# A three-layer kernel on one core: the first phase recorded as steps and emitted by a list scheduler in the kernel

## The chip, the cores and the metric

The kernel runs on one core of a Trainium2 chip. The metric is the device time of one execution in microseconds (us). Engines: TensorE (PE, with PEld for its weight loads), VectorE (DVE), ScalarE (ACT), GpSimd (POOL) and SyncE (SP), which here issues nearly all DMAs. Each engine takes its instructions in the order in which they stand in its program.

## What is computed

```python
s = scale * matmul(p, k.T);  a = exp(s - max);  p_packed = (a / (sum + 1e-9)) @ v
s = scale * matmul(q, p_packed.T);  x = softmax(s) @ p_packed      # 8 batches, 8 heads, 576 x 64
h = max(max(x @ w1, x @ w2), x @ w3);  x2 = h @ w_out              # 4608 x 512 -> 768 -> 512
h = x2 @ w_in;  g = (a0 + a1 h + a2 h^2 + a3 h^3) / (1 + |b0||h| + |b1|h^2 + 1e-6)
out = g @ w_out2                                                   # 4608 x 512 -> 2048 -> 512
```

The weights arrive as 64-bit floats and are turned into pairs (or singles) of 32-bit floats on the chip ("decode"). Each large product is three matmuls: high x high, high x low, low x high (`mm3`, L60).

## The kernel before, in words

Phase one takes the 8 batches in 4 pairs (`bp`). A pair has 4 **units** `u`: two batches `b2`, two groups `g` of four heads. In `place` (L250) the group is the outer index: units 0 to 3 are (g0,b0), (g0,b1), (g1,b0), (g1,b1). A unit goes through these steps, which are named by letters:

- S (`s_stage`, L339): scores of p against k on PE, their maximum on DVE (L350), the exponent on ACT (L359);
- T (`sum_stage`, `a_stage`, L363 and L372): row sums on POOL, reciprocal on DVE (L370), transposes on PE (L377), copy on ACT;
- V, Z (L381 to L400): product with v on PE, scaled on DVE (`zt`, L393), transposed on PE (L399), copied by ACT into `ppk`;
- s (`s2_stage`, L275): scores of q on PE (L283), transposes and sums on DVE, two products with broadcast operands on POOL (L291, L298), exponent on ACT, and the result split into `a2h`, `a2l`.

`m_stage` (L311) multiplies the packed values of one group, both batches, by one decoded weight piece `wt`; its low part `ml` is made on DVE (L326). `y_stage` (L459) does, for one `f` of 6 and one batch, three products `psy` (12 matmuls of 288 columns each, over both groups): the first is copied from PSUM by ACT (L471), the two others are max-ed in by DVE (L473). Two PSUM buffers serve all of them. The result is split into `hh`, `hl`. So a pair has 36 products. `x2_stage` (L480) then does the second layer, 8 times 36 matmuls a pair, from both batches' six `hh`, `hl`.

Decoding a piece (`decode`, L68) is 4 or 5 passes on DVE, 2 or 3 on ACT and one on POOL. In the first pair 12 pieces for the first layer and 4 for the second are decoded; the 12 are kept in DRAM (`w_scr`) and loaded again for later pairs. In pairs 1 to 3 the 32 pieces of phase two are decoded (512 columns each).

What sets the order: the first pair's units and its first decodes follow a hand-written text (`START`, L522) under a manual schedule. From there on, the loops of L533 call steps for the next pair between products (`between`, `PACK`, `SECOND`), and the framework's own scheduler orders all engines.

Phase two (L627 on) is 9 blocks of 512 tokens by 16 chunks: `h_mm`, the rational function on ACT and DVE, `o_mm`. Its first weight tile `wi_0` has a place of its own, so it is loaded before phase one ends.

Of the kernel before, what the change touches and what calls it, by code (L numbers as in the profile page):

```python
# [25 lines left out]
VC = 6  # L26
# [7 lines left out]
def attn_moe_moe2_kernel(  # L34
# [33 lines left out]
    def decode(pl, raw, n, single, pin):  # L68

        hw, lw = raw[:, :, 1], raw[:, :, 0].bitcast(U32)
        t = pl.tile([128, 768], I32, name="dec_t", bufs=2)[:, :n]
        r = pl.tile([128, 768], I32, name="dec_r", bufs=1)[:, :n]
        keep = 0x7FF00000 if single else 0x7FFFFE00
        ins = dve.tensor_scalar(out=t, in0=hw, scalar1=keep, scalar2=None, op0=ALU.bitwise_and)
        if pin:
            tc.keep_in_program_order(ins)
        if single:
            dve.tensor_scalar(out=r, in0=hw, scalar1=0xFFFFF, scalar2=0x100000, op0=ALU.bitwise_and, op1=ALU.bitwise_or)  # L80
        else:
            dve.tensor_scalar(out=r, in0=hw, scalar1=0x1FF, scalar2=None, op0=ALU.bitwise_and)
        act.activation(t, t, AF.Relu, scale=8.0, bias=reb)
        act.activation(r.bitcast(F32), r, AF.Copy, scale=2.0**-20)
        hi, lo = yield
        rf = lo if single else r.bitcast(F32)
        ins = dve.scalar_tensor_tensor(out=rf, in0=lw, scalar=2.0**-52, in1=r.bitcast(F32), op0=ALU.mult, op1=ALU.add)
        if pin:
            tc.keep_in_program_order(ins)
        hib = hi if hi is not None and hi.dtype == I32 else t  # L90
        dve.scalar_tensor_tensor(out=hib, in0=hw, scalar=-0x80000000, in1=t, op0=ALU.bitwise_and, op1=ALU.bitwise_or)  # L91
        if single:
            w = t
        else:
            w = hw
            dve.tensor_scalar(out=w, in0=hib, scalar1=-0x00800000, scalar2=None, op0=ALU.bitwise_and)
            if hib is t:
                act.copy(hi, t.bitcast(F32))
        pool.tensor_tensor(out=lo, in0=rf, in1=w.bitcast(F32), op=ALU.mult)  # L99

    def load_raw(pl, src, bufs):
        n = src.shape[1]
        raw = pl.tile([128, 768, 2] if wide else [128, 768], I32 if wide else F32, name="w_raw", bufs=bufs)[:, :n]
        nc.sync.dma_start(raw.rearrange("p n w -> p (n w)") if wide else raw, src.bitcast(I32) if wide else src)
        return raw

    class Feed:

        def __init__(self, pl, pieces, bufs, first=0, pin=False):
            self.pin = pin
            self.pl, self.pieces, self.bufs, self.raw, self.half = pl, iter(pieces), bufs, [], []
            for _ in range(first):
                self.load()

        def load(self):
            piece = next(self.pieces, None)
            if piece is not None:
                self.raw.append((load_raw(self.pl, piece[1], self.bufs), piece))  # L120

        def start(self):
            if self.raw:
                raw, piece = self.raw.pop(0)
                gen = decode(self.pl, raw, raw.shape[1], piece[3], self.pin) if wide else None
                if gen is not None:
                    next(gen)
                self.half.append((gen, raw, piece))

        def finish(self, load=True):  # L130
            if self.half:
                gen, raw, (tiles, _, then, single) = self.half.pop(0)
                hi, lo = tiles()
                if gen is not None:
                    try:
                        gen.send((hi, lo))
                    except StopIteration:
                        pass
                elif single:
                    act.copy(lo, raw)  # L140
                else:
                    split(hi, lo, raw, lo_eng="pool")
                if load:
                    self.load()
                if then is not None:
                    then()

        def half_step(self, load=True):
            if self.half:
                self.finish(load)  # L150
            else:
                self.start()

        def step(self):
            self.finish()
            self.start()

# [9 lines left out]
    pool.memset(reb, -REBIAS)  # L167

# [13 lines left out]
    rlow = ctx.enter_context(tc.tile_pool(name="rlow", bufs=1, side="right"))  # L182
    wi_0 = rlow.tile([128, 2, 512], F32R, name="wi_0")
    rstack = ExitStack()
    wp = rstack.enter_context(tc.tile_pool(name="wp", bufs=1, side="right"))
    mp = [rstack.enter_context(tc.tile_pool(name=f"mp{x}", bufs=1, side="right")) for x in range(2)]
    hx = bstack.enter_context(tc.tile_pool(name="hx", bufs=2))


    wt_ready, NWT, NW = {}, 4, 12  # L190

    def wt_tile():
        return wp.tile([128, 2, 512], F32, name="wt", bufs=NWT)

    def w_piece(f, g):

        box = []

        def tiles():
            box.append(wt_tile().rearrange("p a b -> p (a b)")[:, :768])  # L200
            wt_ready[2 * f + g] = box[0]
            return None, box[0]

        def keep():
            nc.sync.dma_start(w_scr[f, g], box[0])
# [12 lines left out]

    def again(n):
        if n is not None:  # L220
            wt = wt_tile().rearrange("p a b -> p (a b)")[:, :768]
            nc.sync.dma_start(wt, w_scr[n // 2 % 6, n % 2])
            wt_ready[n] = wt

    def wo_pieces():

        for m in range(4):
            yield (lambda m=m: (wo_h[:, m], wo_l[:, m])), w_out[m], None, False

    def w2_pieces():  # L230

        for i in range(32):
            box = []

            def tiles(box=box):
                box.append(wt_tile())
                hi, lo = (box[0][:, x] for x in range(2))
                return (hi.bitcast(I32) if wide else hi.bitcast(F32R)), lo.bitcast(F32R)

            def keep(box=box, i=i):  # L240
                nc.sync.dma_start(w2_scr[:, :, 512 * i : 512 * i + 512], box[0])

            yield tiles, w_2[i], keep, False
# [6 lines left out]
    def place(u):  # L250

        bp, g, b2 = u // 4, u // 2 % 2, u % 2
        return 2 * bp + b2, g

    last_load = []

    def load_unit(src, u):

        t = kp.tile([128, 4 * 288], F32, name="kt", bufs=NKT)
        last_load[:] = [nc.sync.dma_start(t, src[place(u)])]  # L260
        return t

    a2p = rstack.enter_context(tc.tile_pool(name="a2p", bufs=1, side="right"))
    kp = rstack.enter_context(tc.tile_pool(name="kp", bufs=1, side="right"))

    ppk = a2p.tile([128, 2, 4, 128], F32, name="ppk")
    NKT = 4
# [4 lines left out]
    def soft_tile():  # L272
        return kp.tile([128, S], F32, name="e", bufs=3)

    def s2_stage(u, qt, done):  # L275

        g, b2 = u // 2 % 2, u % 2
        ps = ps_t.tile([128, 2, 512], F32, name="pst")
        for c2 in range(2):
            for h in range(4):  # L280
                x = 32 * (h ^ b2)
                l = slice(64 * c2, 64 * c2 + 64)
                pe.matmul(ps[x : x + 32, c2, :288], lhsT=ppk[l, u // 4 % 2, u % 4, 32 * h : 32 * h + 32],  # L283
                          rhs=qt[l, 288 * h : 288 * h + 288], start=True, stop=True)
# [117 lines left out]
    class Ahead:  # L402
# [8 lines left out]
        def do(self, what):  # L411
# [35 lines left out]
            elif k == "n":  # L447
                self.low()
# [304 lines left out]
```

## Time and profile before

| | us |
|---|---|
| three runs | 1390.1, 1386.04, 1387.13; median 1387.13 |
| profiled execution | 1383.15, its span 1381.4 |
| phase one, first instruction to first matmul of phase two | 584.5 |
| PE busy | 1310.2, 95% of the span |
| DVE busy | 1048.9, 76% |
| ACT, POOL busy | 803.4 and 230.1 |

The page's time by slices shows where PE is not full: the first slices of 34.5 us each, and thin places in phase one; in phase two the slices read 9. Busy times include the pipelined overlap of neighbours, so the sum over a group of instructions can exceed what the engine spent. The profiled execution lies 4 us (0.3%) under the median of the three runs.

### The profile page before, as it was taken

To read this page: it belongs to the slowest core of one execution; us is meant where nothing else is said; L and a number is where in the kernel's file an instruction comes from. 1 tells how busy PE (TensorE), PEld (TensorE's weight loads), DVE (VectorE), ACT (ScalarE), POOL (GpSimd) and SP (SyncE) were. 2 spreads that over 40 slices of the span, in tenths; PEclk is the share of its full clock that TensorE was granted. 3 is DMA by queue.
4 is the path that set the end of the run, shared out by engine and by line. 5 is a ranking of instruction groups with operands and counts; after the bars stand their busy time and mean duration, and the time that the engine had idled before them with its cause. 6 is when DMAs were issued, how large, how long until landed. Compare 5 with 4: busy or idle time off the path is not lost.

```text
span 1381.4 us, 21521 instructions
## 1 busy us (share of the span) xinstructions
PE 1310.2 (95%) x8496; PEld 1088.3 (79%) x8496; DVE 1048.9 (76%) x1634; ACT 803.4 (58%) x1337; POOL 230.1 (17%) x226
## 2 busy tenths in 40 slices
PE   4488999999999989999999999999999999999998
PEld 2277797889778779988888888888888888888886
DVE  4599866665766584188888978889788898888887
ACT  2355534533543253286867767668676686776765
POOL 2332252434433342000100101001010010100000
PEclk9999999999999999999999999999999999999999
DMA  8556545763763272860100101001010010000000
GB/s 279 182 189 226 196 145 183 226 226 134 251 224 119 104 244 102 320 242 1 61 1 9 54 1 61 1 1 61 1 38 24 0 55 0 18 36 0 32 0 31
DMA packets 51556, 140.85 MB, mean 102 GB/s; under 512 B 5632, under 2 KB 5632, under 8 KB 50688
## 3 DMA queue, kind: packets, MB, share of 16 engines
q1 hardware_dynamic: 51168, 138.96, 30.1%
q8 instruction: 66, 1.08, 0.3%
q10 hardware_dynamic: 288, 0.52, 0.1%
q14 instruction: 34, 0.28, 0.1%
HBM read 99.09 MB, written 40.37 MB: 101 GB/s over the span
## 4 chain that ended last, share of the span: by engine, by line
PE 81%; DVE 6%; DMA 4%; issue 1%; POOL 1%; ACT 1%; SPq 0%; POOLq 0%; DVEq 0%; ACTq 0%
PE po L61 10%; PE po L62 10%; PE po L63 10%; PE psh L62 10%; PE psh L61 10%; PE psh L63 9%; PE psy L61 7%; PE psy L63 7%; PE psy L62 7%; DMA w_scr<-wt 3%; PE pst L321 2%; DVE hm L473 1%; DVE wt L91 1%; DVE ml L326 1%; POOL wt L99 1%
## 5 line engine op out<-in xcount | busy, mean ns | idle before, releaser
L61 PE MATMUL po<-wq_b,gh 128*128 128x512 f32 x540 | 212.3, 393 | 0.8 <-ACT gh L54 0.8
L62 PE MATMUL po<-wq_b,gh 128*128 128x512 f32 x540 | 211.3, 391 | 0.0
L62 PE MATMUL psh<-xl,wi_b 128*128 128x512 f32 x540 | 211.0, 391 | 0.0
L63 PE MATMUL psh<-xh,wi_b 128*128 128x512 f32 x540 | 210.6, 390 | 0.0
L61 PE MATMUL psh<-xh,wi_b 128*128 128x512 f32 x540 | 210.6, 390 | 0.0
L652 ACT ACTIVATE hb<-psh,babs 128x512 f32<-128x512 f32 (+1 forms) x145 | 99.5, 686 | 187.3 <-PE psh L63 187.3
L61 PE MATMUL psy<-a2h,mh 128*128 128x288 f32 x576 | 182.8, 317 | 18.4 <-DVE hm L473 10.6
L63 PE MATMUL po<-wq_b,gl 128*128 128x512 f32 x540 | 181.7, 391 | 0.0
L655 DVE SCALAR_TENSOR_TENSOR hb<-h,babs,hb 128x512 f32<-128x512 f32 (+1 forms) x145 | 108.2, 746 | 96.7 <-ACT h L653 96.5
L63 PE MATMUL psy<-a2h,ml 128*128 128x288 f32 x576 | 173.2, 301 | 8.3 <-DVE ml L326 8.3
L62 PE MATMUL psy<-a2l,mh 128*128 128x288 f32 x576 | 172.8, 300 | 0.0
L61 PEld LDWEIGHTS psy<-a2h,mh 128*128 128x128 f32 x576 | 111.0, 193 | 53.1 <-DVE hm L473 22.1
L58 POOL TENSOR_TENSOR xl<-xr,xh 128x512 fp32r<-128x512 f32 x28 | 36.4, 1299 | 632.5 <-ACT xh L54 632.5
L63 PEld LDWEIGHTS po<-wq_b,gl 128*128 128x128 f32 x540 | 101.3, 188 | 24.0
L61 PEld LDWEIGHTS po<-wq_b,gh 128*128 128x128 f32 x540 | 101.4, 188 | 22.9 <-ACT gh L54 1.2
L63 PEld LDWEIGHTS psy<-a2h,ml 128*128 128x128 f32 x576 | 111.0, 193 | 10.5 <-DVE ml L326 9.5
L62 PEld LDWEIGHTS po<-wq_b,gh 128*128 128x128 f32 x540 | 101.4, 188 | 22.4
L61 PEld LDWEIGHTS psh<-xh,wi_b 128*128 128x128 f32 x540 | 101.4, 188 | 22.1
L62 PEld LDWEIGHTS psh<-xl,wi_b 128*128 128x128 f32 x540 | 101.4, 188 | 21.7
L63 PEld LDWEIGHTS psh<-xh,wi_b 128*128 128x128 f32 x540 | 101.4, 188 | 21.7
L61 PE MATMUL psy<-hh,wo_h 128*128 128x288 f32 x384 | 114.5, 298 | 0.0
L654 ACT ACTIVATE u<-psh,av 128x512 f32<-128x512 f32 (+1 forms) x145 | 113.3, 782 | 1.6 <-DVE gl L58 1.6
(105 smaller groups left out, 2754.0 us busy)
## 6 DMA issues: line engine op xcount, KB each, us to landing
w_raw<-in_w_dram SPq DMA_DIRECT2D x32, 512.0 KB, 3.9
w_scr<-wt SPq DMA_DIRECT2D x32, 512.0 KB, 5.0
wt<-w_scr SPq DMA_DIRECT2D x36, 384.0 KB, 4.1
kt<-in_k_dram SPq DMA_DIRECT2D x16, 576.0 KB, 4.6
vraw<-in_v_dram SPq DMA_DIRECT2D x16, 576.0 KB, 5.9
kt<-in_q_dram SPq DMA_DIRECT2D x16, 576.0 KB, 6.2
w_raw<-in_w_dram SPq DMA_DIRECT2D x12, 768.0 KB, 4.6
x_scr<-hm SPq DMA_DIRECT2D x32, 288.0 KB, 2.5
```

The lines of the kernel that those rows point to most:

```text
L58: e.tensor_tensor(out=lo, in0=src, in1=hi.bitcast(F32), op=ALU.subtract)
L61: pe.matmul(out_ap, lhsT=lh, rhs=rh, start=first, stop=False)
L62: pe.matmul(out_ap, lhsT=lh, rhs=rl, start=False, stop=False)
L63: pe.matmul(out_ap, lhsT=ll, rhs=rh, start=False, stop=last)
L91: dve.scalar_tensor_tensor(out=hib, in0=hw, scalar=-0x80000000, in1=t, op0=ALU.bitwise_and, op1=ALU.bitwise_or)
L99: pool.tensor_tensor(out=lo, in0=rf, in1=w.bitcast(F32), op=ALU.mult)
L321: pe.matmul(ps[c : c + 32, b2, :384], lhsT=ppk[l, bp % 2, 2 * g + b2, 32 * h : 32 * h + 32], rhs=wt[l, 384 * i : 384 * i + 384], start=Tru ...
L326: return lambda: dve.tensor_tensor(out=lo, in0=ps[:, :, :384], in1=hi.bitcast(F32), op=ALU.subtract)
L473: dve.tensor_tensor(out=hm, in0=ps[:, :, :288], in1=hm, op=ALU.max)
L652: act.activation(hb, h, AF.Abs, scale=babs[:, 0:1])
L654: act.activation(u, h, AF.Identity, scale=av[:, 3:4], bias=av[:, 2:3])
L655: dve.scalar_tensor_tensor(out=hb, in0=h2, scalar=babs[:, 1:2], in1=hb, op0=ALU.mult, op1=ALU.add)
```

## The change

All of phase one up to the last pair's third-layer input is no longer issued as it is written. Each step is recorded by `add(engine, us, fn, r, w, up, mode, kb)`: an engine, a duration, a function that issues its instructions, what it reads and writes, and a rank. `Plan.run` then picks step after step, under a manual schedule: of all engines the one whose next step can start first by the recorded durations, and on it, among steps within a look-ahead of that start, the lowest rank. Evictions from PSUM have their rank lowered (`up=OUT`, `2 * OUT`), so they go first. Steps marked `two` on DVE and POOL are taken as excluding one another. Tiles come from rings (`Buf`); a step can't be issued before the old tile's users are.

```diff
+        def run(self):
+            free = dict.fromkeys(("PE", "DVE", "ACT", "POOL", "SP"), 0.0)
...
+                            t = max(free[e], op.ready)
+                            for b in op.bufs:
+                                s = b.since()
...
+                    near = [(op.rank, t, op) for t, op in found if t <= first + LOOK[e]]
+                    best = (first, *min(near, key=lambda x: x[:2])[1:])
...
+                elif e == "SP":
+                    dma = max(dma, t + 2.0) + op.kb / 406.0
+                    end, free[e] = dma, t + 0.45
+                else:
+                    if op.mode == "two":
+                        t = max(t, held["POOL" if e == "DVE" else "DVE"])
+                        held[e] = t + op.us
+                    end = t + op.us
+                    free[e] = end - 0.08
+                op.fn()
...
+    LOOK = {"PE": 0.1, "DVE": 0.3, "ACT": 0.2, "POOL": 0.1, "SP": 0.1}
...
+            add("DVE", 0.2 + 0.75 * k, low, r=[raw, rb], w=[rb], mode="two")
+            add("DVE", 0.2 + 0.75 * k, sign, r=[raw, tb], w=[tb, key], mode="two")
...
-        bp, g, b2 = u // 4, u // 2 % 2, u % 2
+        bp, b2, g = u // 4, u // 2 % 2, u % 2
...
+        add("PE", 1.6, mm, r=[mh, ml, *a2[0], *a2[1]], w=[ps])
+        if w == 0:
+            add("ACT", 0.65, lambda: act.copy(hm(), ps()[:, :, :288]), r=[ps], w=[hm], up=2 * OUT)
+        else:
+            add("DVE", 0.76, lambda: dve.tensor_tensor(out=hm(), in0=ps()[:, :, :288], in1=hm(), op=ALU.max),
+                r=[ps, hm], w=[hm], up=2 * OUT)
...
+    YS = [[(f, b2) for f in range(6) for b2 in range(2)] for bp in range(NBP)]
+    YS[0] = [(0, 0), (1, 0), (0, 1), (1, 1)] + YS[0][4:]
...
+    START = "P L0 L1 W0 l0 R R W1 l1 S0 S1 T0 T1 V0 V1 s0 s1 L2 L3 W2 W3 l2 l3 R d m S2 S3 T2 T3 V2 V3 s2 s3 R R R d m m"
...
+    with tc.manual_schedule():
+        plan.run()
+    for t, src in ((av, a_in), (bv, b_in)):
+        nc.sync.dma_start(t, src.partition_broadcast(128))
+    dve.tensor_scalar(out=babs, in0=bv, scalar1=-1.0, scalar2=None, op0=ALU.mult)
+    dve.tensor_tensor(out=babs, in0=babs, in1=bv, op=ALU.max)
```

Beside it: a pair's units are ordered by batch, and `m_stage` takes one batch, both groups and both weight pieces of `f`; in the first pair the products of batch 0 for f 0 and 1 stand ahead of batch 1's. The pass that sets a bit of the mantissa with a second operation (L80) loses it; ACT's conversion (L84) adds 1.0 instead. `hm` has 3 buffers instead of 2. `wi_0` loses its own place: all 16 first weights of phase two are loaded into the room that phase one frees. The last pair's second layer and phase two are still ordered by the framework, as is the preparation of `babs` after the plan.

On PE at the start, before: the first product (rows `psy`) stands behind units 0 to 2 in part (`kt,pt` is S; `ident,e` T; `vraw,at` V; `ident,zt` Z; `kt,ppk` s; `wt,ppk` m).

```order
L377 MATMUL pst<-ident,e 96x128 x6
L347 MATMUL pst<-kt,pt 32x288 x8
L388 MATMUL pst<-vraw,at 32x64 x24
L399 MATMUL pst<-ident,zt_111 128x128
L283 MATMUL pst<-kt,ppk 32x288 x8
L321 MATMUL pst<-wt,ppk 32x384 x8
L377 MATMUL pst<-ident,e 96x128 x6
L61 MATMUL psy<-a2h_315,mh 128x288
L62 MATMUL psy<-a2l_316,mh 128x288
```

The same place now:

```order
L475 MATMUL pst<-kt,ppk 32x288 x16
L526 MATMUL pst<-wt,ppk 32x384 x8
L393 MATMUL pst<-kt,pt 32x288 x16
L434 MATMUL pst<-ident,e 96x128 x12
L452 MATMUL pst<-vraw,at 32x64 x24
L460 MATMUL pst<-ident,zt_108 128x128
L452 MATMUL pst<-vraw,at 32x64 x24
L60 MATMUL psy<-a2h_412,mh 128x288
L61 MATMUL psy<-a2l_456,mh 128x288
L62 MATMUL psy<-a2h_412,ml 128x288
```

Units go in twos (x16, x12), batch 0 is whole before the first product, and the product has its low weight part `ml` from the start.

On DVE at the start, now (L266 to L285 are decode; L457 is `zt`; L483, L495 belong to s):

```order
L266 TENSOR_SCALAR dec_t<-w_raw 128x768
L269 TENSOR_SCALAR dec_r<-w_raw 128x768
L457 TENSOR_SCALAR zt_109<-pst,sm 128x128
L723 TENSOR_SCALAR babs<-bv 128x2
L724 TENSOR_TENSOR babs<-babs,bv 128x2
L285 SCALAR_TENSOR_TENSOR dec_t<-w_raw,dec_t 128x768
L278 SCALAR_TENSOR_TENSOR wt<-w_raw,dec_r 128x768
L483 STREAM_TRANSPOSE e<-pst 128x288 x4
```

The two `babs` rows have come here from the third pair (L541 before); their load now stands tenth in SP's queue, behind 6016 KB of p, k, v, q and weight loads.

A little later on DVE, before and then now, where the first two PSUM evictions of products stand (L473, now L551):

```order
L301 STREAM_TRANSPOSE hm<-e 128x576
L473 TENSOR_TENSOR hm<-psy,hm 128x576
L87 SCALAR_TENSOR_TENSOR wt<-w_raw,dec_r 128x768
L58 TENSOR_TENSOR a2l_587<-hm,a2h_586 128x576
L76 TENSOR_SCALAR dec_t<-w_raw 128x768
L80 TENSOR_SCALAR dec_r<-w_raw 128x768
L473 TENSOR_TENSOR hm<-psy,hm 128x576
```

```order
L285 SCALAR_TENSOR_TENSOR dec_t<-w_raw,dec_t 128x768
L507 TENSOR_TENSOR a2l_589<-hm,a2h_587 128x576
L504 STREAM_TRANSPOSE hm<-e 128x576
L551 TENSOR_TENSOR hm<-psy,hm 128x576 x2
L507 TENSOR_TENSOR a2l_625<-hm,a2h_612 128x576
L559 TENSOR_TENSOR hl_638<-hm,hh_627 128x576
L531 TENSOR_TENSOR ml<-pst,mh 128x768 x2
```

In both, nearly all of the four units' DVE work stands ahead of these rows; now the next two `ml` follow at once.

## Rows read from the trace of the kernel before

**Rows 1.** Stretches by stage: start, first products, pairs' products and second layers.

```profile
core 0: us, PE busy (x) PEld busy (x) DVE busy (x) ACT busy (x) POOL busy (x), PEclk, DMA share, GB/s
0.00:34.80 34.80, 14.84 (x211) 7.85 (x212) 14.45 (x31) 10.23 (x22) 7.49 (x21) 1.00 0.87 279
34.80:68.60 33.80, 13.39 (x181) 7.65 (x178) 19.18 (x36) 10.45 (x18) 9.93 (x15) 0.94 0.53 183
68.60:163.50 94.90, 84.72 (x904) 69.33 (x910) 86.91 (x121) 50.93 (x84) 27.86 (x29) 0.97 0.64 211
163.50:205.50 42.00, 42.00 (x359) 39.13 (x341) 28.29 (x45) 16.49 (x24) 20.93 (x14) 1.00 0.42 145
205.50:290.50 85.00, 81.79 (x910) 67.68 (x916) 53.76 (x94) 38.63 (x72) 28.61 (x34) 1.00 0.59 190
...
332.10:422.50 90.40, 85.97 (x910) 69.69 (x916) 64.82 (x114) 44.50 (x80) 34.21 (x38) 0.96 0.62 203
...
464.10:545.20 81.10, 73.83 (x594) 62.02 (x593) 58.37 (x87) 33.80 (x52) 30.74 (x22) 0.98 0.48 157
545.20:584.50 39.30, 38.36 (x290) 38.15 (x289) 7.19 (x10) 8.44 (x14) 0.00 (x0) 1.00 0.88 314
```

**Rows 2.** The same view for tile psy alone, products of pair 1, then of pair 3.

```profile
205.50:290.50 85.00, 63.33 (x434) 58.06 (x432) 18.23 (x25) 7.64 (x12) 1.00 0.59 190
...
464.10:545.20 81.10, 63.60 (x434) 59.47 (x433) 18.04 (x24) 7.65 (x12) 0.98 0.48 157
```

**Rows 3.** PE's timeline: start us, us, instruction, [idle before it <- who ended that].

```profile
6.34 1.22 PE L347 MATMUL pst<-kt,pt 64*32 64x288 f32 x16 [6.34 <-DMA kt<-in_k_dram]
...
34.88 0.59 PE L61 MATMUL psy<-a2h,mh 128*128 128x288 f32 x1
...
68.63 0.61 PE L63 MATMUL psy<-a2h,ml 128*128 128x288 f32 x1 [6.47 <-DVE ml L326]
...
70.96 0.44 PE L62 MATMUL psy<-a2l,mh 128*128 128x288 f32 x1
...
77.30 0.30 PE L62 MATMUL psy<-a2l,mh 128*128 128x288 f32 x1
...
584.51 0.47 PE L61 MATMUL psh<-xh,wi 128*128 128x512 f32 x1 [0.94 <-DVE hm L489]
```

**Rows 4.** DVE's groups of instructions from 0 to 165.6 us, shapes apart.

```profile
L473 DVE TENSOR_TENSOR hm<-psy,hm 128x576 f32<-128x576 f32 x24 | 18.0, 748 | 2.0 <-ACT dec_t L83 1.0 <-PE psy L63 0.9
L58 DVE TENSOR_TENSOR hl<-hm,hh 128x576 fp32r<-128x576 f32 x12 | 16.0, 1337 | 3.2 <-ACT hh L54 3.1
L80 DVE TENSOR_SCALAR dec_r<-w_raw 128x768 int32<-128x768 int32 x12 | 12.2, 1014 | 0.0
```

**Rows 5.** Timeline around 143 us: DVE and POOL.

```profile
143.15 1.83 POOL L99 TENSOR_TENSOR wt<-wt,dec_t 128x768 f32<-128x768 f32 x1
...
143.28 2.32 DVE L58 TENSOR_TENSOR hl<-hm,hh 128x576 fp32r<-128x576 f32 x1
```

**Rows 6.** DVE's timeline: the same operations when they ran alone.

```profile
70.67 0.55 DVE L80 TENSOR_SCALAR dec_r<-w_raw 128x768 int32<-128x768 int32 x1
...
152.63 0.76 DVE L58 TENSOR_TENSOR hl<-hm,hh 128x576 fp32r<-128x576 f32 x1 [0.27 <-ACT hh L54]
```

**Rows 7.** DMA of the first 60 us: GB/s in 40 slices of 1.5 us.

```profile
GB/s 0 109 293 350 249 339 424 397 348 242 350 424 277 258 182 6 265 304 356 397 243 225 364 410 413 390 70 228 349 240 127 200 196 3 11 225 168 123 391 268
```

**Rows 8.** Waits of PE and PEld (engine, line, waited for: us, times, longest), 205.5 to 584.5 us.

```profile
PEld psy L61 <- DVE hm L473: 18.1, 21, 2.5
...
PE psy L61 <- DVE hm L473: 8.9, 9, 2.3
```

**Rows 9.** ACT's timeline: last of the four casts that phase two's first block needs.

```profile
576.84 0.62 ACT L54 CAST xh<-xr 128x512 fp32r<-128x512 f32 x1
```

**Rows 10.** Groups of instructions whose recorded duration in the plan is shorter.

```profile
L87 DVE SCALAR_TENSOR_TENSOR dec_r<-w_raw,dec_r 128x512 f32<-128x512 uint32 x32 | 27.8, 869 | 9.1 <-ACT dec_r L84 8.8
L58 POOL TENSOR_TENSOR hl<-hm,hh 128x576 fp32r<-128x576 f32 x33 | 47.9, 1451 | 72.7 <-ACT hh L54 68.9 <-DMA w_raw<-in_w_dram 3.5
```

More of the change, by code (lines that the diff above doesn't have):

```diff
@@ L101, in load_raw @@
[L101 to L156, printed above, removed]
@@ L219, in again @@
[L219 to L243, printed above, removed]
+    mp = rstack.enter_context(tc.tile_pool(name="mp", bufs=4, side="right"))
@@ new lines, in s_stage @@
+        add("PE", 0.58, mm, r=[kt, ("pt", 0), ("pt", 1)], w=[ps], mode="t")
+        add("DVE", 0.75, lambda: dve.tensor_reduce(out=mx()[:, 0:2], in_=ps()[:, :, :288], axis=AX.X, op=ALU.max),
+            r=[ps], w=[mx], up=OUT)
+        add("DVE", 0.6, small, r=[mx], w=[mx], up=OUT)
+        add("ACT", 1.38, exps, r=[ps, mx], w=[e, sm], up=OUT)
+        add("POOL", 0.9, sums, r=[sm], w=[sm])
+        add("DVE", 0.2, lambda: dve.reciprocal(out=sm()[:, 4:5], in_=sm()[:, 3:4]), r=[sm], w=[sm])
+        return e, sm
@@ new lines, in x2_out, with x2_store, x2_stage @@
+    def x2_out(b, m, ps, xs):
+        (act.copy if m < 3 else dve.tensor_copy)(xs, ps[:, :, :288])
+    def x2_store(b, m, xs):
+        nc.sync.dma_start(x2_scr[:, m, S * b : S * b + S], xs.rearrange("p a b -> p (a b)"))
+    def x2_stage(b, m, hs):
+        ps, xs = ps_buf("psy"), hm_buf()
+        for half in range(2):
+            add("PE", 2.38, lambda half=half: x2_mm(ps(), m, half, hs),
+                r=[("wo", m), *(x for h in hs for x in h), *([ps] if half else [])], w=[ps])
+        add("ACT" if m < 3 else "DVE", 0.7, lambda: x2_out(b, m, ps(), xs()), r=[ps], w=[xs], up=2 * OUT)
+        add("SP", 0, lambda: x2_store(b, m, xs()), r=[xs], kb=288)
@@ new lines, in attn_moe_moe2_kernel, with m_next, wo_next @@
+    YS = [[(f, b2) for f in range(6) for b2 in range(2)] for bp in range(NBP)]
+    YS[0] = [(0, 0), (1, 0), (0, 1), (1, 1)] + YS[0][4:]
+    m_made = []
+    m_seq = iter([(bp, f, b2) for bp in range(NBP) for f, b2 in YS[bp]])
+    def m_next():
+        got = next(m_seq, None)
+        if got is not None:
+            bp, f, b2 = got
+            m_made.append(got)
+            ms[got] = m_stage(bp, b2, wts[bp, f])
+    wo_seq, w2_seq = iter(range(4)), iter(range(32))
+    def wo_next():
+        m = next(wo_seq, None)
+        if m is not None:
+            decode(raw_ready.pop(("o", m)), False, lambda: (wo_h[:, m], wo_l[:, m]), ("wo", m))
@@ new lines, in attn_moe_moe2_kernel @@
+    loads = [(wi_at(f), f) for f in range(16)] + [(wq_at(f), 16 + f) for f in range(NQA)]
+    per = -(-len(loads) // 8)
+    for b2 in range(2):
+        for m in range(4):
+            for _ in range(min(per, len(loads))):
+                tiles, o = loads.pop(0)
+                load_w2(tiles, o, 1)
+            if (b2, m) == (0, 2):
+                xc = load_x(0, xpa)
+            ps = ps_y.tile([128, 2, 512], F32, name="psy")
+            for half in range(2):
+                x2_mm(ps, m, half, hs[b2])
+            xs = hx.tile([128, 2, 288], F32, name="hm", bufs=3)
+            x2_out(2 * bp + b2, m, ps, xs)
+            x2_store(2 * bp + b2, m, xs)
```

751 lines of the change are left out of this document (417 added, 334 removed), and 3 rows, old and new, of the table SECOND.

## The prediction

> **What bounds the kernel now.** I read the stretches by stage first, since phase two is left alone and only phase one's 584.5 us can move. In [rows 1] the reader takes, for each stretch, its length less PE's and DVE's busy time. In the first two stretches (68.6 us) PE is idle for 40.4 us. In the third, the first pair's products, PE is idle for 10.2 of 94.9 us and DVE works 86.91: here DVE is the bound. In the products of pairs 1, 2 and 3 DVE is idle for 31, 26 and 23 us and PE for 3.2, 4.4 and 7.3: PE is the bound, with holes. In the second layer of a pair (42.0 us) PE has no idle time.
>
> PE's timeline comes next [rows 3]. The first product starts at 34.88 us, stops after a few matmuls, and goes on at 68.63, when the low weight part is there. So 68.6 us pass with less than one of 36 products done. The DVE groups and two pieces of the timeline tell what DVE's time is made of [rows 4 to 6]: a subtraction `hl` takes 0.76 us alone, but 1.337 on average, and 2.32 when it starts 0.13 us after a POOL product of 1.83 us.
>
> **The first pair.** The sum is made on DVE, because it decides when the last product can be finished. Up to 163.5 us it was busy for 14.45 + 19.18 + 86.91 = 120.5 us and idle for 20.4 + 14.6 + 8.0 = 43 us [rows 1]. What does the change do to each?
>
> Work. The order is new, the instructions nearly the same. The pass that loses its second operation gains nothing: it took 0.55 us with two operations when it ran alone [rows 6]; its mean of 1014 ns [rows 4] is waiting for POOL, 12 x 0.46 = 5.6 us in all, and so is 12 x 0.58 = 6.9 us of `hl`. I leave both in. One more piece of the second layer's weight is decoded before the last product (four passes of 0.55 to 0.9 us, [rows 6, 10]: 3 us), and the `babs` rows move here (two small passes, 1 us). Work: 124.5 us.
>
> Idle time. It is bounded below by the first load: PE's first matmul waits until 6.34 us [rows 3], so DVE starts near 8, and above by today's 43 us. I go through the new order. DVE's first 15 rows are some 6.5 us of work. Then stands `babs`, whose load is behind 6016 KB. By the rates of [rows 7], whose slices I add up, that much has landed at 21 us. So DVE is idle for about 15 us by then; without `babs` the row behind it would wait for the second v tile, which lands after some 4.9 MB, near 17 us, and the s step of it, so the wait for `babs` itself costs 2 to 4 us. Next the two units of batch 0 go through s together, and each pass over POOL and ACT leaves DVE with decodes and with batch 1's scores to do; I allow 6 us for the two round trips. For the products proper I take 4 us (8.0 before in 94.9 us). Together 25 us, much nearer to 43 than to 8, because half of the four units' chain cannot be hidden.
>
> So the last product of the first pair ends near 124.5 + 25 = 149.5 us instead of 163.5: **14 us gained**. On the way, the first product should start near 44 us (all of batch 0 stands ahead of it), three are done by 54, and the next waits for `ml`, which on DVE stands behind nearly all four units' work: near 67 us. PE is then idle again and has fallen to the lower level of its clock; the same matmul took 0.44 us at 70.96, after such a wait, and 0.30 at 77.30 [rows 3]. From 67 on, PE needs less than DVE: about 33 products of 63.33 / 36 = 1.76 us [rows 2] and what stood between them, against 78 us of DVE work. Bounds: no gain at all (idle time as before) and 32 us (idle 8 us and some waiting for loads).
>
> **Pairs 1 to 3.** Here PE counts. Pairs 1 and 2 issue the same matmuls; pair 1 took 81.79 us of PE, pair 2 85.97, part of it at the lower clock (0.96 granted over the stretch) [rows 1]. I take pair 1's busy time for both and 2.5 us of holes, since evictions now go first: 84.3 instead of 85.0 and 90.4, so 0.7 and 6.1 gained. Pair 3 has no units to prepare. Its products took 63.60 us of `psy` [rows 2], though they are interrupted half as often as pair 1's 63.33; I take 60, plus 8 for the weight products instead of 73.83 - 63.60 = 10.2, plus 2.5 of holes: 70.5 instead of 81.1, 10.6 gained. At the seams the next products may fill in between second-layer halves; about 1 us a seam, 3 in all. Sum: **20 us**. Bounds: 0, if the holes come back elsewhere, and 28, with no holes and no waits in the weight products.
>
> **Edits at nothing.** `wi_0` is no longer loaded ahead. That puts 512 KB more into the last stretch, which has the DMA engines at 0.88 and moves 314 GB/s [rows 1]: 1.7 us. The fourth input cast of phase two was done at 577.5 and phase two began at 584.5 [rows 3, 9], so 7 us cover it; if that cover is gone, phase two starts up to 2 us late. The third `hm` buffer takes away a wait on stores and adds no instruction. Other pieces of the order on SP only move loads that are issued several us before use.
>
> **The sum** against the profiled execution: 1383.15 - 14 - 20 = 1349. That execution lies 4 us under the median of the three runs, against which I forecast: 1387.1 - 34 = **1353 us**.
>
> **The rivals.** First, no waiting on POOL: if the plan's `two` rule really keeps DVE and POOL apart, the 5.6 + 6.9 us of [rows 4, 6] go as well: 1353 - 12.5 = 1340. For it: the plan knows of the exclusion. Against it: it delays the later step in its own account, and doesn't choose another in its place. The Trainium skill (SBUF — State Buffer, "Who interferes with whom") says that a VectorE instruction with two inputs in SBUF and a GpSimd instruction that reads it hold the shared port in turn, and that the one issued first keeps it for its whole length; the 2.32 us of [rows 5] agree (1.83 less 0.13 waiting, then the own pass). By that rule an order alone saves only what it keeps from meeting.
>
> Second, the first pair doesn't move: DVE is 92% busy in the third stretch, and what is won at the start may be lost to evictions behind decodes. Then only the 20 us are left: 1367. Third, the later pairs don't move, because PE there is nearly full: 1373.
>
> Fourth, on the other side, **evictions come late**. The order is fixed by durations that are too short in places: a decode pass is entered at 0.70 us and took 0.869, a POOL subtraction at 1.25 and took 1.451 [rows 10]. An eviction that stands behind two such passes is late, and with two PSUM buffers a product of 1.76 us leaves only about 1 us over the eviction's 0.748 [rows 2, 4]. Before, PE and its weight loads waited 27 us for these evictions in the last three pairs [rows 8]. The 144 products lose the whole gain when each waits 34 / 144 = 0.24 us longer; at 0.35 us it is 50 us, and 1387 + 16 = 1403. Against it: on the order, evictions stand soon behind their products, and DVE has 23 to 31 us free in each of these pairs.
>
> **Chances.** The forecast's own case 0.50 (1340 to 1364), less waiting on POOL 0.15, only the later pairs 0.15, only the first pair 0.09, late evictions 0.07, no change at all 0.04. Differences within 0.3%, 4 us, are what a measurement of this kernel cannot tell from none. So faster 0.89, same 0.04, slower 0.07. The range from 1331 to 1375 takes in the first three rivals and the bounds of the larger terms; it leaves out the last two cases and the tail of a gain over 56 us.
>
> **What would show it.** First product near 44 us, a gap to about 67, last product of the first pair near 150, with DVE idle for about 25 us until then; pairs 1 and 2 at 84 us of products each and pair 3 near 70; second layers still 41 to 42 us; phase two 797 us long. I am wrong in the first step if DVE's busy time until the first pair's end grows, in the second if PE's holes in the later pairs stay above 4 us each, and wholly if waits of `psy` for `hm` exceed today's 27 us.

## The result and the profile after

| | before | after |
|---|---|---|
| runs, median us | 1386.59 (1385.61 to 1390.1, 4 runs) | 1333.1 (1332.61 to 1333.96, 4 runs) |
| profiled execution, its span | 1383.15, 1381.4 | 1332.61, 1330.4 |
| phase one | 584.5 | 533.4 |
| phase two | 796.9 | 797.0 |
| PE, DVE busy | 1310.2, 1048.9 | 1290.6, 1068.5 |

The ratio after to before is 0.9611 (95% interval 0.9593 to 0.9628): 53.5 us faster, where 34 were forecast. The profiled execution of before lay under its median, so between the two traces there are 51.0 us of span, and all of it lies in phase one. The stretches of the changed kernel, with the columns of [rows 1]:

```profile
core 0: us, PE busy (x) PEld busy (x) DVE busy (x) ACT busy (x) POOL busy (x), PEclk, DMA share, GB/s
0.00:41.20 41.20, 22.31 (x331) 12.25 (x331) 26.36 (x54) 17.47 (x35) 13.73 (x32) 1.00 0.96 316
41.20:65.00 23.80, 16.27 (x158) 11.52 (x151) 19.55 (x32) 9.16 (x14) 9.37 (x6) 0.78 0.75 223
65.00:140.90 75.90, 69.48 (x793) 59.16 (x791) 70.40 (x104) 43.87 (x74) 23.76 (x25) 1.00 0.69 230
140.90:184.80 43.90, 43.33 (x386) 39.58 (x386) 37.83 (x56) 20.73 (x31) 25.60 (x17) 1.00 0.45 146
184.80:263.30 78.50, 78.34 (x878) 66.27 (x876) 61.88 (x96) 39.21 (x72) 31.75 (x35) 1.00 0.73 231
...
303.50:383.80 80.30, 80.30 (x912) 68.99 (x910) 64.09 (x100) 41.14 (x74) 33.36 (x36) 1.00 0.64 204
...
424.10:494.10 70.00, 70.00 (x612) 62.08 (x611) 42.27 (x64) 29.50 (x44) 26.07 (x18) 1.00 0.42 134
494.10:533.40 39.30, 38.39 (x290) 38.16 (x288) 6.45 (x9) 7.63 (x12) 0.00 (x0) 1.00 0.90 320
533.40:1330.40 797.00, 791.63 (x3456) 648.54 (x3456) 673.13 (x1020) 562.34 (x935) 36.91 (x28) 1.00 0.10 33
```

Three things are to be seen. The first pair's products end at 140.9 instead of 162.6 (the stage of [rows 1] is cut a little later, at 163.5), and with its second layer 20.7 us are won by 184.8. From there to 533.4 PE has no idle time worth naming, where before 14.6 us of waits stood in pairs 1 to 3: beside the 8.9 us of [rows 8] mainly these:

```profile
PE psy L61 <- ACT hm L471: 1.7, 2, 1.3
PE pst L321 <- issue: 1.6, 1, 1.6
PE pst L321 <- ACT e L359: 1.1, 1, 1.1
```

And the products of pair 1 take 78.5 us, less than the 81.79 that PE was *busy* with them before [rows 1]. Some of that is only moved: 878 matmuls stand in the stretch instead of 910, because two steps of weight products now come before it (about 1.6 us). Pair 2's products have 912, and take 80.3 us. Pair by pair, with the seam behind it, the time from first product to first product fell from 126.6 to 118.7, from 132.0 to 120.6 and from 120.4 to 109.3 us: 7.9, 11.3 and 11.1.

The first products on PE's timeline (columns as in [rows 3]):

```profile
41.26 0.61 PE L60 MATMUL psy<-a2h,mh 128*128 128x288 f32 x1
...
54.78 0.61 PE L60 MATMUL psy<-a2h,mh 128*128 128x288 f32 x1 [7.44 <-ACT hm L549]
...
60.71 0.53 PE L60 MATMUL psy<-a2h,mh 128*128 128x288 f32 x1
```

The first product starts later than before (41.26 against 34.88), but goes through; one long wait is left, for ACT's copy out of PSUM, and from 60.7 on products follow regularly, where before they resumed at 68.63. On ACT that copy (54.10 us) stands behind the cast of batch 1's `a2h` (L505, 53.52 us), which had waited 2.69 us for DVE's transposition: in this place the plan put an eviction behind another step's chain.

What ended PE's waits from 184 to 534 us (columns as in [rows 8]) is a single row, the first matmul of phase two:

```profile
PE psh L60 <- issue: 1.0, 1, 1.0
```

DVE's groups in the first pair, 0 to 141 us (columns as in [rows 4]):

```profile
L551 DVE TENSOR_TENSOR hm<-psy,hm 128x576 f32<-128x576 f32 x23 | 17.2, 750 | 3.7 <-PE psy L62 3.4
L285 DVE SCALAR_TENSOR_TENSOR dec_t<-w_raw,dec_t 128x768 int32<-128x768 int32 x15 | 14.7, 987 | 0.8 <-ACT dec_t L272 0.8
L266 DVE TENSOR_SCALAR dec_t<-w_raw 128x768 int32<-128x768 int32 x15 | 13.6, 904 | 0.0
L269 DVE TENSOR_SCALAR dec_r<-w_raw 128x768 int32<-128x768 int32 x14 | 12.7, 906 | 0.0
...
L559 DVE TENSOR_TENSOR hl<-hm,hh 128x576 fp32r<-128x576 f32 x11 | 9.9, 903 | 1.3 <-ACT hh L557 1.2
```

Two rows of before, for 0 to 163 us, go with them:

```profile
L58 DVE TENSOR_TENSOR hl<-hm,hh 128x576 fp32r<-128x576 f32 x11 | 15.3, 1390 | 3.2 <-ACT hh L54 3.1
L76 DVE TENSOR_SCALAR dec_t<-w_raw 128x768 int32<-128x768 int32 x14 | 8.8, 630 | 0.6 <-DMA w_raw<-in_w_dram 0.6
```

Eleven subtractions `hl` went from 15.3 us to 9.9, and the first pass of a decode (L76, now L266) from 630 ns to 904. All decode passes together are 59 up to the last product in both kernels, and took 53.0 us before and 54.8 now.

Last, PE's small groups in pairs 1 to 3, first before (205.5 to 584.5 us), then after (184.8 to 533.4); m is the product with a weight piece, the other rows V and S:

```profile
L321 PE MATMUL pst<-wt,ppk 64*32 64x384 f32 x544 | 36.5, 497 | 3.5 <-issue 1.6 <-ACT e L359 1.1 <-PE pst L321 0.9
L388 PE MATMUL pst<-vraw,at 96*32 96x64 f32 x384 | 9.3, 228 | 0.0
L347 PE MATMUL pst<-kt,pt 64*32 64x288 f32 x128 | 7.6, 413 | 0.0
```

```profile
L526 PE MATMUL pst<-wt,ppk 64*32 64x384 f32 x528 | 29.0, 493 | 0.0
L452 PE MATMUL pst<-vraw,at 96*32 96x64 f32 x384 | 7.0, 221 | 0.0
L393 PE MATMUL pst<-kt,pt 64*32 64x288 f32 x128 | 5.7, 413 | 0.0
```

One matmul of m lasts as long as before (497 and 493 ns), the group is a fifth cheaper, though it has 16 matmuls fewer, one step, which now stands ahead of the stretch (0.8 us). So what changed is how many of them run beside each other. This the prediction had not seen. Groups that stand wound into each other are counted twice in these busy times. Counted from each matmul's start to the next instruction's, without idle time, m fell by some 7 us, V by 2.0 and S by 0.9.

### The profile page after: what moved, and what is told of

It is laid out like the page before. It is cut to its first block, busy times and chain, and to the rows that moved or that the text cites. A ratio compares the mean times of both kernels' runs of the same rounds, so it can differ in the third digit from the quotient of the medians.

```text
span 1330.4 us, 21496 instructions
## 1 busy us (share of the span) xinstructions
PE 1290.6 (97%) x8496; PEld 1080.3 (81%) x8496; DVE 1068.5 (80%) x1634; ACT 801.7 (60%) x1337; POOL 243.1 (18%) x226
## 4 chain that ended last, share of the span: by engine, by line
PE 93%; DVE 3%; DMA 2%; ACT 2%; issue 0%; SPq 0%; POOL 0%; ACTq 0%; DVEq 0%; POOLq 0%
PE psy L60 10%; PE po L60 10%; PE po L61 10%; PE po L62 10%; PE psh L60 10%; PE psh L61 10%; PE psh L62 10%; PE psy L62 9%; PE psy L61 9%; PE pst L526 3%; DMA bv<-in_moe_b_dram 1%; PE pst L452 1%; PE pst L393 1%; PE pst L475 1%; DMA vraw<-in_v_dram 1%; PE pst L434 1%
## 5 line engine op out<-in xcount | busy, mean ns | idle before, releaser
L60 PE MATMUL psh<-xh,wi_b 128*128 128x512 f32 x576 | 224.4, 390 | 1.0 <-issue 1.0
L61 PE MATMUL psh<-xl,wi_b 128*128 128x512 f32 x576 | 224.9, 390 | 0.0
L62 PE MATMUL psh<-xh,wi_b 128*128 128x512 f32 x576 | 224.6, 390 | 0.0
L60 PE MATMUL psy<-a2h,mh 128*128 128x288 f32 x576 | 178.8, 310 | 7.5 <-ACT hm L549 7.4
L60 PEld LDWEIGHTS psy<-a2h,mh 128*128 128x128 f32 x576 | 109.3, 190 | 35.7 <-issue 17.8
L60 PEld LDWEIGHTS psh<-xh,wi_b 128*128 128x128 f32 x576 | 108.1, 188 | 24.5 <-issue 1.2
L62 PEld LDWEIGHTS psh<-xh,wi_b 128*128 128x128 f32 x576 | 108.1, 188 | 23.0
L61 PEld LDWEIGHTS psh<-xl,wi_b 128*128 128x128 f32 x576 | 108.1, 188 | 23.0
L53 ACT CAST gh<-u 128x512 fp32r<-128x512 f32 (+1 forms) x145 | 90.7, 626 | 41.6 <-DVE u L801 40.4
L799 DVE SCALAR_TENSOR_TENSOR u<-u,av,h 128x512 f32<-128x512 f32 (+1 forms) x145 | 109.0, 751 | 7.6 <-ACT h L796 7.6
```

What stands on the lines that cost most here:

```text
L53: act.copy(hi, src)
L60: pe.matmul(out_ap, lhsT=lh, rhs=rh, start=first, stop=False)
L61: pe.matmul(out_ap, lhsT=lh, rhs=rl, start=False, stop=False)
L62: pe.matmul(out_ap, lhsT=ll, rhs=rh, start=False, stop=last)
L799: dve.scalar_tensor_tensor(out=u, in0=u, scalar=av[:, 0:1], in1=h2, op0=ALU.add, op1=ALU.mult)
```

## The experiments

My theory after the result: the list order does it, and three of its rules carry it (recorded durations, evictions first, DVE and POOL kept apart). The rivals: the new arrangement of the units, or the early products of the first batch, do it; or DVE's work alone sets the first pair. All edits are made to the changed kernel.

**The same steps, the framework's order.** The steps are issued as they were recorded, and the framework orders the engines.

```diff
-    with tc.manual_schedule():
-        plan.run()
+    for o in plan.ops:
+        o.fn()
...
```

> The same steps in the order in which they are recorded, without a manual schedule: the framework's scheduler orders them, as it ordered nearly all of the kernel before. Batch order, products, buffers and passes are those of the change. Theory, by which the list order makes most of the gain: 25 us or more of the 53 are lost, 1358 to 1387. Rival, by which the new arrangement of the work makes it: within 8 us of 1333.

1380.98 us, ratio 0.9959 (0.9942 to 0.9976). Windows by pair: the first pair's products, its second layer, then pairs 1, 2 and 3.

```profile
0.00:162.30 162.30, 109.31 (x1296) 81.82 (x1297) 130.71 (x208) 78.17 (x132) 54.87 (x66) 0.97 0.71 232
162.30:204.70 42.40, 42.40 (x361) 39.23 (x360) 20.45 (x37) 13.75 (x21) 16.85 (x13) 1.00 0.44 153
204.70:340.60 135.90, 127.17 (x1259) 107.27 (x1258) 88.25 (x150) 55.31 (x97) 51.86 (x51) 1.00 0.62 200
340.60:473.10 132.50, 124.94 (x1256) 106.63 (x1255) 91.31 (x151) 56.47 (x98) 52.45 (x51) 1.00 0.54 176
473.10:581.90 108.80, 107.89 (x876) 98.22 (x874) 48.98 (x69) 36.17 (x55) 24.46 (x17) 1.00 0.54 186
```

Its waits of PE in phase one begin with evictions:

```profile
PE psy L60 <- DVE hm L551: 13.8, 17, 1.8
```

The first pair ends at 162.3, as before the change, pair 1 is longer than before and pair 2 as long; only pair 3 keeps the gain. The new arrangement alone is worth 6 of the 53 us; with the list order come the other 48. In this run the framework also orders the start, which before stood in a hand-written order; how much of the 48 that is in the first pair wasn't tried apart.

**Flat durations.** The list scheduler stays, but each engine has one duration for all its steps.

```diff
+            us = {"PE": 1.2, "DVE": 0.7, "ACT": 0.7, "POOL": 1.3, "SP": 0}[eng]
```

> The plan with one duration for every step of an engine: PE 1.2, DVE 0.7, ACT 0.7, POOL 1.3 us. Ranks, rings, look-ahead and loads stay. Theory, by which the order is good because its times are near the chip's: the holes come back, 10 to 25 us, 1343 to 1358. Rival, by which any order that fills an engine with ready steps and puts evictions first does it: within 5 us, up to 1338.

1363.41 us, 0.9829 (0.9811 to 0.9846): 30 us slower than the change, more than the theory's 25. The loss is spread: the first pair's products end at 149.3 (8.4 later), its second layer takes 47.0, and each later pair 5 to 6 us more. Pairs 2 and 3:

```profile
320.80:447.30 126.50, 120.42 (x1176) 106.30 (x1175) 91.40 (x148) 52.39 (x93) 52.59 (x48) 0.97 0.57 185
447.30:561.70 114.40, 107.70 (x884) 100.14 (x883) 58.85 (x82) 39.25 (x61) 28.82 (x19) 1.00 0.59 207
```

PE is idle for 6 us in each again. So without durations by kind more than half of what the scheduler brings is lost.

**More exact durations.** The POOL steps that were entered too short get their measured times.

```diff
-            add("POOL", 0.1 + 1.7 * k, mul, r=[tb, key], w=[key], mode="two")
+            add("POOL", 0.1 + 1.9 * k, mul, r=[tb, key], w=[key], mode="two")
...
-        e, us = (dve, 0.78) if lo_eng == "dve" else (pool, 1.25)
+        e, us = (dve, 0.78) if lo_eng == "dve" else (pool, 1.45)
...
```

> The plan with POOL's durations as the changed kernel's trace has them: decode products 0.1 + 1.9 k instead of 1.7 k, low parts 1.45 instead of 1.25 and 1.3, the subtraction 1.35 instead of 1.2 us. Theory, by which evictions hardly came late: within 3 us of 1333. Rival, by which too short prices still cost the later pairs something: 4 us or more gained, 1329 or less.

1336.38 us, 0.9634 (0.962 to 0.9649): no gain, 3 us the other way, all of it behind the first pair, whose products end at the same 140.9. Errors of 11 to 16% in POOL's durations cost nothing here; with all kinds alike it cost 30 us.

**Evictions not ahead.** They keep the rank of their place.

```diff
-    OUT = 100000
+    OUT = 0
```

> The plan without priority for evictions: OUT is 0, so each step's rank is its place in the record. Theory, by which evictions that go first close PE's holes: the holes and slow weight products of pairs 1 to 3 come back, and the first pair waits too: 10 to 25 us more, 1343 to 1358. Rival, by which the look-ahead and the times do it and ranks hardly matter: within 4 us of 1333.

1342.32 us, 0.9666 (0.9636 to 0.9696): 9 us lost, just under what the theory said, and in another place. (The four executions lie between 1336.7 and 1343.7, and the profiled one is the longest of them.) The first pair's products end 13 us later, at 154.0, with DVE at 119.9 us of work and idle for 34.1 us instead of 24.6; PE waits there for evictions by DVE, as it did not in the change (last row, columns as in [rows 8]):

```profile
0.00:41.20 41.20, 18.80 (x231) 9.82 (x232) 23.07 (x50) 13.88 (x29) 12.15 (x28) 0.93 0.96 307
41.20:154.00 112.80, 96.54 (x1057) 77.92 (x1057) 96.83 (x145) 60.14 (x98) 34.46 (x37) 0.85 0.66 217
...
PE psy L60 <- DVE hm L551: 7.7, 3, 5.3
```

The first pair's second layer gives some 3 us of it back, and the later pairs run as in the change (119.5, 121.0 and 109.3 us with their seams). There DVE has over 20 us free in each pair, and it seems that an eviction finds it free without a rank.

**DVE and POOL not kept apart in the plan.**

```diff
-                    if op.mode == "two":
-                        t = max(t, held["POOL" if e == "DVE" else "DVE"])
-                        held[e] = t + op.us
```

> The plan no longer takes DVE's and POOL's two-input steps as excluding each other; it computes with times that are too early where they meet. Theory: the account only corrects times, the order hardly moves, and the chip's own waiting is the same: within 5 us of 1333. Rival: knowing of the exclusion is what lowered DVE's busy time in the first pair (116 against 120 us), so DVE's busy time there rises by 5 us or more, and the time to 1340 or more.

1345.96 us, 0.9706 (0.9675 to 0.9737): 13 us lost (four executions from 1342.0 to 1350.3, the profiled one 1343.5), but not where the rule was thought to work: the time is the rival's, its reason is not. The first pair ends at 140.1, as early as with it; DVE works 3.2 us more there (119.5 against 116.3) and is idle for less. Pairs 1 and 2 lose, 7.1 and 5.2 us:

```profile
182.80:308.60 125.80, 121.66 (x1262) 105.98 (x1262) 93.42 (x151) 56.84 (x98) 54.03 (x52) 1.00 0.67 218
308.60:434.40 125.80, 121.66 (x1262) 105.99 (x1261) 93.07 (x151) 56.83 (x98) 53.71 (x51) 1.00 0.56 186
...
PE psy L60 <- ACT hm L568: 4.7, 2, 2.3
PE psy L60 <- DVE hm L548: 4.5, 8, 1.1
```

DVE is no busier than in the change (95.4 and 97.1 us), but PE waits 4.1 us in each for evictions; the last two rows are its waits in all three later pairs. The other 3 us of pair 1 are matmuls that stood ahead of it in the change (1262 against 1228). That the plan then places the evictions of DVE and ACT by times that DVE can't keep is my reading; it wasn't tried apart.

**The first pair's `hl` on POOL.** If DVE's work alone sets the first pair, its end must move with it.

```diff
-            hs[b2][f] = y_end(b2, f, hm, "dve" if bp == 0 or (b2, f) == (1, 5) else "pool")
+            hs[b2][f] = y_end(b2, f, hm, "dve" if (b2, f) == (1, 5) else "pool")
```

> In the first pair the low parts hl are made on POOL instead of DVE, as in the later pairs. DVE was busy for 70.4 of 75.9 us from 65 to 141 us, POOL for 23.8. Theory, by which DVE bounds the first pair: 10 passes of 0.76 to 0.9 us leave DVE, of which 4 to 7 us come through: 1326 to 1329. Rival, by which the two engines' excluding each other eats it (POOL's pass takes 1.45 us): within 2 us of 1333.

1335.55 us, 0.9624 (0.9608 to 0.964): no gain, and not to be told from the change. (The profiled execution, 1339.17, is the longest of the four.)

```profile
0.00:41.20 41.20, 21.38 (x323) 11.92 (x327) 26.17 (x54) 17.39 (x35) 13.57 (x31) 0.90 0.96 314
41.20:145.50 104.30, 88.90 (x944) 72.45 (x937) 87.02 (x124) 54.04 (x88) 49.97 (x43) 0.91 0.67 213
...
L285 DVE SCALAR_TENSOR_TENSOR dec_t<-w_raw,dec_t 128x768 int32<-128x768 int32 x14 | 17.5, 1250 | 0.8 <-ACT dec_t L272 0.8
```

DVE's work to the end of the first pair falls from 116.3 to 113.2 us, POOL's rises from 46.9 to 63.5, and the end comes 4.6 us later, at 145.5. Eleven subtractions left DVE, but only 3 us of work: a decode pass there (L285) went from 987 ns to 1250. The theory of DVE alone falls, by which 1326 to 1329 should have come. That DVE and POOL together set the pair's end is a reading of these rows; no run shows it apart.

**Units in the old order.** Batches alternate again; the plan stays.

```diff
+            i = (0, 2, 1, 3)[i] if k in "LWlSTVs" else i
...
```

> The plan stays, but a pair's units alternate between the batches again (b0, b1, b0, b1), as before the change; at the start the first weight product moves behind all four units' s steps in the record. If the batch order is what shortens the start (rival), the first product comes near 58 us instead of 41, DVE's idle time in the first pair goes back to some 43 us, and the 20 us of the first pair are lost: 1353 us. If the list order makes the gain and the batch order only helps (theory), DVE has other work to take and the loss is 5 to 10 us: 1338 to 1343.

1335.91 us, 0.9636 (0.9617 to 0.9655): less lost than either expectation said. The first product starts at 49.0 instead of 41.3, the first pair's products end at 144.8 instead of 140.9: of nearly 8 us at the start 4 are left at the end. The order by batch is worth some 3 us at most; the two intervals overlap.

**The first batch's products not ahead.**

```diff
-    YS[0] = [(0, 0), (1, 0), (0, 1), (1, 1)] + YS[0][4:]
```

> In the first pair the products alternate between the batches from the start; batch 0's product of f 1 no longer stands ahead of batch 1's first. Theory, by which DVE's work sets the first pair's end: under 3 us, 1333 to 1336. Rival, by which the early products of batch 0 shorten the start: the second product waits for batch 1's whole chain, 5 us or more, 1338 to 1345.

1334.57 us, 0.9631 (0.9611 to 0.965): the first pair ends at 143.4, and the time is not to be told from the change. The losses of this run and of the one before add up to under 5 us; the two edits weren't tried together.

**Other loads at the start.** The second v tile is loaded ahead of a weight piece, and `babs` is made in the last pair, so that DVE doesn't wait for it.

```diff
-    START = "P L0 L1 W0 l0 R R W1 l1 S0 ...
+    START = "P L0 L1 W0 W1 R l0 l1 R S0 ...
...
```

> The load of the second v tile stands ahead of the first q and the second weight piece, and the two small loads with the babs passes are recorded in the last pair. In the changed kernel PE waited 2.5 us for that v tile, and DVE 0.6 us for bv. Theory: the start is a chain of loads and of the first two units, so the first product comes 2 to 3 us earlier than 41.3 us; DVE's work decides the pair's end, so 0 to 3 us come through: 1330 to 1333. Rival, by which each us at the start counts in full or more: 1329 or less.

1338.3 us, 0.9644 (0.9623 to 0.9666): slower by 5 us; both expectations missed.

```profile
0.00:41.20 41.20, 15.24 (x206) 7.09 (x206) 23.22 (x41) 14.07 (x24) 11.70 (x23) 1.00 0.91 293
41.20:146.70 105.50, 93.37 (x1065) 75.87 (x1066) 94.70 (x148) 56.51 (x98) 33.66 (x39) 0.92 0.68 225
```

DVE does 23.2 us of work in the first 41.2 instead of 26.4, because the second weight piece, which it could have decoded, comes later: its first decode pass starts at 27.0 us instead of 18.8. PE's weight products wait 13.9 us for decoded pieces up to 60 us, so the first product starts at 43.3, 2 us later instead of 2 to 3 earlier; the end of the first pair moves from 140.9 to 146.7. The run makes two edits at once, but the other one can't explain much: in the change DVE waits 0.6 us for the load of `babs`.

**The look-ahead.** First longer on PE, then none anywhere.

```diff
-    LOOK = {"PE": 0.1, "DVE": 0.3, "ACT": 0.2, "POOL": 0.1, "SP": 0.1}
+    LOOK = {"PE": 0.6, "DVE": 0.3, "ACT": 0.2, "POOL": 0.1, "SP": 0.1}
```

> PE's look-ahead is 0.6 us instead of 0.1: PE rather waits half a us for a step of lower rank than it takes another at once. Theory, by which PE in pairs 1 to 3 is without holes and every wait there is a loss: 2 to 8 us more, 1335 to 1341. Rival, by which fewer changes between kinds of matmul pay for the waits: up to 3 us less, 1330.

1331.49 us, 0.9599 (0.9581 to 0.9617): not to be told from the change, though the theory said 2 to 8 us more.

```diff
-    LOOK = {"PE": 0.1, "DVE": 0.3, "ACT": 0.2, "POOL": 0.1, "SP": 0.1}
+    LOOK = {"PE": 0.0, "DVE": 0.0, "ACT": 0.0, "POOL": 0.0, "SP": 0.0}
```

> No look-ahead on any engine: the step that can start first goes first, rank decides only between equals. Theory, by which the look-ahead on DVE (0.3 us) lets an eviction go ahead of a pass that is ready a little earlier: 3 to 10 us more, 1336 to 1343, with waits of products for evictions. Rival, by which ranks among steps ready at once do it all: within 2 us of 1333.

1337.92 us, 0.9644 (0.9625 to 0.9662): 5 us lost, as the theory had it. The first pair's products end 1 us later (142.0), which its second layer makes up for; pairs 1 and 2 lose 5.0 and 2.9 us, and pair 3 gains 2.5.

**Steps cut in two.** This last run is for PE's own time in pairs 1 to 3, which the prediction had taken as fixed. The weight products and V are recorded as two halves each, the second ranked behind the next product.

```diff
-        add("PE", 0.74, mm, r=[*wts, ...
+            add("PE", 0.37, lambda: mm([0]), r=[*wts, ("ppk", bp % 2, 2 * b2)], w=[ps], mode="t")
+            add("PE", 0.37, lambda: mm([1]), r=[*wts, ("ppk", bp % 2, 2 * b2 + 1)], w=[ps], mode="t", up=-12)
...
+            add("PE", 0.34, lambda: mm(range(3)), r=[at, vt], w=[ps], mode="v")
+            add("PE", 0.34, lambda: mm(range(3, VC)), r=[at, vt], w=[ps], mode="v", up=-8)
```

> In pairs 1 to 3 the weight products (m) and the products with v (V) are recorded as two halves, the second ranked behind the next product, so that PE takes 54 pieces of four m matmuls and 22 halves of V where the change has whole steps; everything else is the change. In pairs 1 to 3 of the kernel before, m took 36.5 us for 544 matmuls and V 9.3 us for 384; with the change 29.0 for 528 and 7.0. If it is the splitting that cost this (some 16 pieces of m, 12 of V before, so 0.3 to 0.5 us a piece), then halving all of them costs more than it did before: m 36 us or more, V 9 us or more, pairs 1 to 3 longer by 8 to 20 us, 1341 to 1353 us in all. If instead the difference was waits of single matmuls inside the groups in the old order, m stays within 29 to 32 us and V within 7 to 8, and the time within 1333 to 1338 us.

1370.98 us, 0.9885 (0.9864 to 0.9905): 38 us slower than the change, far more than expected: pairs 1 to 3 grew by 27.8 us, where the theory said 8 to 20. The two groups in pairs 1 to 3, to be held against those above:

```profile
L530 PE MATMUL pst<-wt,ppk 64*32 64x384 f32 x528 | 51.8, 493 | 0.3
L452 PE MATMUL pst<-vraw,at 96*32 96x64 f32 x384 | 8.7, 223 | 0.0
```

The weight products take 51.8 us instead of 29.0, for the same 528 matmuls of 493 ns. Why, PE's timeline shows: first a place in this run, then one in the change, then one before.

```profile
362.02 0.85 PE L530 MATMUL pst<-wt,ppk 64*32 64x384 f32 x8
```

```profile
335.57 0.88 PE L526 MATMUL pst<-wt,ppk 64*32 64x384 f32 x16
```

```profile
338.51 0.45 PE L347 MATMUL pst<-kt,pt 64*32 64x288 f32 x4
338.54 0.55 PE L321 MATMUL pst<-wt,ppk 64*32 64x384 f32 x4
338.78 0.42 PE L347 MATMUL pst<-kt,pt 64*32 64x288 f32 x4
338.88 0.96 PE L321 MATMUL pst<-wt,ppk 64*32 64x384 f32 x12
```

A step of m, eight matmuls in the program, is sixteen in the trace, two **sets** of eight. The eight of a set start within 0.05 us and end within 0.05 us of each other, and the second set starts 0.35 us behind the first. A half step is eight in the trace, in two sets of four, and these stand 0.35 us apart as well: a half step takes as long as a whole one (0.85 and 0.88 us). So PE pays by the set, nearly whatever is in it. Counting the sets in pairs 1 to 3 and summing the time from each m matmul's start to the next instruction's: 68 sets and 26.6 us with the change, 86 sets and 33.6 us before, 126 sets and 47.5 us here. Both differences come to nearly the same price, 7.0 / 18 = 0.39 and 20.9 / 58 = 0.36 us a set; the first may hold some of the lower clock, at which part of pair 2 ran before. The theory's 0.3 to 0.5 us a piece is thus the price of a set, and a half step has two of them: that it had not counted. In the order of before seven of the 34 steps were cut, or wound into S as in the last rows; the other 27 stood whole. The Trainium skill (TensorEngine Tiling (Array Packing), "Key Properties") has it that different tiles of the array can execute matmuls in parallel; the 64*32 in these rows is such a tile, and the trace agrees.

Of the 36 us that phase one grew, 21 are these sets, 1 is V, 2 are waits and 3.5 are in the products and second layers of pairs 1 to 3. The first pair's end (146.6 instead of 140.9) and its second layer (46.5 instead of 43.9) took 8 more, though their own steps aren't cut; why stays open.

## Why the prediction was right, and where its sum was not

The time fell into the range and the direction was right; the gain was 20 us larger than the sum said. Of these 20, 6.7 are in the first pair and 10.3 in pairs 1 to 3; the rest is that the profiled execution of before lay further under its median than that of the change.

- **First pair: 14 forecast, 20.7 found by the end of its second layer.** The idle time came out as worked, part by part: 14.84 + 4.25 + 5.50 = 24.6 us of DVE against 25, with 13.4 us by 22.2 us (15 forecast), 5.7 up to 65.0 (6) and 5.5 from there (4). Only the wait for `babs` was smaller, 0.6 us instead of 2 to 4. The work did not come out: 26.36 + 19.55 + 70.40 = 116.3 us against 124.5. Two steps failed. One is "one more piece of the second layer's weight", put at 3 us: the decode passes ahead of the last product are 59 in both kernels, and `babs` took 0.3 us instead of 1. The other is "I leave both in", the waits for POOL inside DVE's passes: the eleven `hl` fell by 5.4 us. Not all of that was saved: the decode passes took 1.8 us more, the first of them (L266) a mean of 904 ns instead of 630. So the rival of less waiting on POOL held for less than 4 of its 12.5 us. Whether DVE's work is the whole bound stays open: with `hl` on POOL it fell by 3.1 us, and the pair ended later in the profiled execution.
- **The way there.** The first product was forecast for 44 and came at 41.3. Then the prediction had three products and a gap for `ml` from 54 to 67; it was two, and a gap from 47 to 54.8 for ACT's copy. Products resumed at 60.7 instead of 67.
- **Holes in pairs 1 to 3: 2.5 us a pair forecast, none found.** Before, PE's waits in these pairs came to 14.6 us, of which 8.9 for DVE's evictions [rows 8]. This is 7.4 of the 10.3 us by which the three pairs missed, and the larger part of it.
- **PE's own time there.** Pairs 1 and 2 gained 7.9 and 11.3 us, seams included, where 0.7 and 6.1 and 1 us a seam were forecast. Beside the holes, the step that failed is "I take pair 1's busy time for both". Busy time was taken as a floor; it held the cut sets. Without idle time, m, V and S fell by some 10 us in the three pairs with no matmul faster, and the run with cut steps raised m again by 22.8 us busy. The product groups fell by 5.9 us, in pairs 2 and 3 alone, where the granted clock had been 0.96 and 0.98 [rows 1] and is 1.00 now; for pair 2 the forecast had this in.
- **Pair 3: 10.6 forecast, 11.1 found** with its seam; 70.5 forecast for its products, 70.0 found. The products and weight products came out as worked (59.2 and 8.3 us for 60 and 8). That the total fits as well is luck: in place of the 2.5 us of holes stand 2.5 us of second-layer matmuls of pair 2.
- **Late evictions** (the other side): not one wait of a product or of its weight loads for `hm` in pairs 1 to 3, against 27 us before [rows 8]. Longer durations for POOL changed nothing for the better, so the short entries were harmless.
- **Edits at nothing** came out so: the last second layer took 39.3 us as before with 320 GB/s of loads, phase two 797.0 us.

What the scheduler brings, by the runs: 48 of 53 us against the framework's order with the same steps; without the durations 30 of them go, without DVE and POOL kept apart 13, without ranks 9, without look-ahead 5. These are taken out one at a time; they add up to more than 48, so their effects overlap. No version tried beats the change beyond its interval.

## What to carry to other kernels

An engine's busy time is no floor where small matmuls run side by side: look at the groups of one operation, compare the time of the group with that of one instruction, and see whether steps that belong together are cut. For a list scheduler written into a kernel, durations by kind of step matter more than their last tenth, and steps should be recorded as whole as the hardware takes them. Where two engines hold each other up, count what their waits cost in the new order, not in the old one.

## What the runs showed of the hardware

A set of m matmuls costs PE 0.36 to 0.39 us, with four matmuls in it as with eight. Waits of DVE beside POOL move between passes: a pass over integers with one operand from SBUF (L80 before, L269 now) took 0.55 us alone [rows 6] and 0.906 on average in the change, and with `hl` on POOL a decode pass rose from 987 to 1250 ns. Bringing one load forward came with a loss of 5 us: the DMA engines were at 0.96 of their time in the first 41 us of the change, and the second weight piece was decoded 8 us later for it.
